# Three narrow token chunks instead of five, and one d_ff tile to two attention steps in a new order

## The chip, the core and the metric

The kernel runs on one core of a Trainium2 chip. The metric is the device time of one execution in microseconds (us). The engines are PE (TensorE, the matrix engine; PEld is its weight load), DVE (VectorE), ACT (ScalarE), POOL (GpSimd) and SP (SyncE, which issues most of the DMAs).

## What is computed

Three layers follow one another, all in float32 precision. Tokens are 4 x 576 = 2304; heads are 8 of 64 columns.

```python
def phi(x):                                   # q, k times 64 ** -0.25
    h = einsum('bhsd,md->bhsm', x, omega) - sum(x * x) / 2
    return exp(h - max(h)) / sqrt(128)
kv = einsum('bhsm,bhsd->bhmd', phi(k), v);  z = sum_s phi(k)
x = einsum('bhsm,bhmd->bhsd', phi(q), kv) / (einsum('bhsm,bhm->bhs', phi(q), z) + 1e-6)
...
h = x @ w_in                                  # d_model 512, d_ff 2048
y = (max(h, 0) + alpha * min(h, 0)) @ w_out
...
out = ((y @ w_a) * (y @ w_b)) @ w_out2        # d_ff 1536
```

## The kernel before, in words

The attention is cut into 40 key tiles: units u (four heads of one batch, 8 of them) times t (five tiles of 128 tokens, the last of 64). A step s takes one key tile and, some steps later, one query tile. Its pieces are named by their PSUM or SBUF tiles:

- `pp(u, t)`: projections of a key and a query tile (`a_proj`), then the row maxima `nm` on DVE (`a_max`) and eight exponentials `ph` on ACT (`a_exp`);
- `kv`: the state product of a key tile (`a_kv`). After a unit's fifth tile ACT copies the state to `kvp`;
- `tp`: the transposes of the features of a query tile (`a_t`), copied to `phT`;
- `nd`: numerators and denominators from `phT` and `kvp` (`a_num`), which DVE divides into `xn`;
- `xp`: transposes of `xn` (`a_x`), copied to the tokens' columns `xT`.

The second layer runs beside the attention on tokens whose `xT` is there. Its weights arrive packed; a decoder (class `Decoder`, object `D_`) unpacks them piece by piece: `r` on ACT, `a` and a custom operation on DVE, `w` on ACT, the low part on POOL. `Mlp.split` makes a high and a low part (`xh`, `xl`) of a chunk. One d_ff tile f (of 16) is `h`, 12 matmuls of 128 columns of w_in, then u, gh and gl on ACT and DVE, then `y`, 12 matmuls into the output's banks, kept for the whole chunk.

The narrow object `A` has chunks of `CI` = 256 tokens, of which there are `NCI` = 5, and does the first 8 d_ff tiles of each. The wide object `X` has chunks of 512. In phase 0 it does the first 8 d_ff tiles of the tokens that `A` leaves (`REST`), in phase 1 the last 8 tiles of all tokens. A narrow h is 12 matmuls of 256 columns, a wide one 12 of 512. The third layer follows.

The order on each engine is the order in which the program calls its parts (a manual schedule); pools of buffers add waits for what was in a buffer before. PSUM has 8 banks: five in a ring for pp, tp, nd, xp and h of the narrow part (tag "ps"), one for kv, two for y. `xn` and `phT` have two buffers each.

Steps 0 to 14 are attention alone. Then `A.run(work0, ..., stop=ALONE)` puts one attention step inside each d_ff tile, for the first `ALONE` = 4 entries of the list `work0` (chunk, its d_ff tiles). After these `group(fronts, at)` takes two attention steps and two d_ff tiles: both state products, numerators and x transposes of earlier groups come first (`wait` holds them), then the two projections, then the two feature transposes with y of the group before (`back_one`) between them, then h (`whole`). When the attention is over the rest of `line` runs alone, then `over()` makes the wide object.

Of the kernel before, what the change touches and what calls it, by code (L numbers as in the profile page):

```python
# [23 lines left out]
KT = DM // P  # L24
# [8 lines left out]
WARM = 11  # L33
Q_LAG = 6
CI = 256
NCI = 5
NF0 = 8
NFH = 5
CB = 512
REST = (512, 512)  # L40
CHUNKS = (512, 512, 256, 512, 512)
NS = 25
NS1 = 17
# [15 lines left out]
PACE2 = 1  # L59
PACE3 = 1  # L60
FIRST = 32
ALONE = 4
LAND = 5.0
SIDE = 0

# [2 lines left out]
def tile_kernel(ctx: ExitStack, tc: tile.TileContext, qT, kT, v1, omT, wbits, alpha, out):  # L68
# [411 lines left out]
    class Mlp:  # L480
        def __init__(self, st, cap, ybufs, side=None):
            self.cap = cap
            self.pair = 2 * cap <= 512
            pool = lambda **kw: st.enter_context(tc.tile_pool(side=side, reuse_waits="tile" if side else "pool", **kw))

            if not self.pair:
                self.px = pool(name=f"px{cap}", bufs=6)
            self.xs, self.ys, self.gs, self.part = {}, {}, {}, {}
            self.half = {}
            self.q = []  # L490
            self.beside = None
            self.seen = set()
            self.after = []
            self.open_ = lambda: self.rest(pool, ybufs)
            if self.pair:
                self.open_()

        def rest(self, pool, ybufs):
            cap = self.cap
            self.pg = pool(name=f"pg{cap}", bufs=3)  # L500
            self.pu = pool(name=f"pu{cap}", bufs=2 if self.pair else 1)
            self.io = pool(name=f"io{cap}", bufs=1)
            if self.pair:
                self.px = pool(name=f"px{cap}", bufs=8)
            self.banks = lambda h=None: self.open(pool, ybufs, h)

# [94 lines left out]
        def a_back(self, ph, o, n, f, last_chunk):  # L601
            halves = self.pair and o < 2 * CI
            first = f in (0, NF0) or (halves and f == NFH)
            last = f in (NF0 - 1, FA - 1) or (halves and f == NFH - 1)
            if first:
                if self.pair:
                    ts = [self.psy.tile([P, 2, 256], F32, tag="y", name=f"y{ph}_{o}_{e}") for e in range(2)]
                    self.ys[o] = [ts[e // 2][:, e % 2, :n] for e in range(KT)]
                else:
                    self.ys[o] = [self.psy.tile([P, 512], F32, tag="y", name=f"y{ph}_{o}_{e}")[:, :n]  # L610
                                  for e in range(KT)]
            ys = self.ys[o]
            wh, wl = hilo(2 * f + 1)
            gh, gl = self.gs.pop((ph, o, f))
            kinds = ((wh, gh), (wl, gh), (wh, gl))
            for e, i in [(e, i) for part in ((0, 1), (2,)) for e in range(KT) for i in part] if self.pair else \
                    [(e, i) for e in range(KT) for i in (0, 2, 1)]:
                es = slice(e * P, (e + 1) * P)
                head = not self.pair or e % 2 == 0
                tail = not self.pair or e % 2 == 1  # L620
                w_, r_ = kinds[i]
                end = 2 if self.pair else 1
                tensor.matmul(ys[e], lhsT=w_[:, es], rhs=r_,
                                 start=(first and i == 0 and head), stop=(last and i == end and tail))
                if i == end and not self.pair and e < 3 and not last:
                    D_.fill()
            D_.free[2 * f + 1] = last_chunk
            if last:
                if halves and f == NFH - 1:

                    yh = xT[:, :, 3 * S + o:3 * S + o + n]
                    for e in range(KT):
                        if e % 2:
                            vector.tensor_copy(yh[:, e], ys[e])
                        else:
                            nc.scalar.activation(yh[:, e], ys[e], AF.Copy)
                    self.half[o] = yh
                elif halves:
                    yo = self.half.pop(o)
                    for e in range(KT):  # L640
                        vector.tensor_tensor(out=yo[:, e], in0=ys[e], in1=yo[:, e], op=ALU.add)
                    nc.sync.dma_start(out=ypart[:, :, o:o + n], in_=yo)
                elif ph == 0:
                    yo = self.io.tile([P, KT, self.cap], F32, tag="io", name=f"yo{o}")[:, :, :n]
                    for e in range(KT):
                        if e % 2:
                            vector.tensor_copy(yo[:, e], ys[e])
                        else:
                            nc.scalar.activation(yo[:, e], ys[e], AF.Copy)
                    nc.sync.dma_start(out=ypart[:, :, o:o + n], in_=yo)  # L650
                else:
                    yp = self.part.pop(o)
                    for e in range(KT):
                        vector.tensor_tensor(out=yp[:, e], in0=ys[e], in1=yp[:, e], op=ALU.add)
                    nc.sync.dma_start(out=ypart[:, :, o:o + n], in_=yp)
                self.ys.pop(o)

        def load_y(self, o, n):
            yp = self.io.tile([P, KT, self.cap], F32, tag="io", name=f"yp{o}")[:, :, :n]
# [181 lines left out]
    def a_t(u, t):  # L841

        ns = slots_of(t)
        ph = phiq.pop((u, t))
        pp = bank(f"tp{u}_{t}").rearrange("p (o m) -> p o m", m=P)
        for h in range(ns):
            tensor.transpose(pp[:, h, :], ph[:, h, :], ident)
        d = pq.tile([P, 4, P], F32, tag="phT", name=f"phT{u}_{t}", bufs=2)
        if pick({"act": 0.1 + 0.13 * ns}, {"dve": 0.1 + 0.15 * ns}):
            vector.tensor_copy(d[:, :ns], pp[:, :ns])  # L850
        else:
            nc.scalar.activation(d[:, :ns], pp[:, :ns], AF.Copy)
        phT[u, t] = d
# [23 lines left out]
    def a_x(u, t, into=None):  # L877
# [10 lines left out]
            tensor.transpose(xp[:, 0, :], xn[:, 0], ident)  # L888
            xp = xp[:, 0, :].rearrange("p (a n) -> p a n", a=2)
        dst = xT[:, 2 * g:2 * g + 2, b * S + t * P:b * S + t * P + n]  # L890
        if pick({"act": 0.2 + n / 600}, {"dve": 0.1 + n / 480}):
            vector.tensor_copy(dst, xp)
        else:
            nc.scalar.activation(dst, xp, AF.Copy)
# [3 lines left out]
    done = {"kv": set(), "x": set()}  # L898
    late = {1: 3, 2: 3, 3: 4, 4: 5}
    own_banks = (0, 3, *range(6, SPLIT_AT, 2))  # L900
    held = {}
    for i, ut in enumerate((u, t) for u in range(U) for t in range(TT)):
        ev["k"][i] = ut
        ev["kv"][i + 1] = ut
# [110 lines left out]
    with st_m:  # L1015
# [38 lines left out]
        def group(fronts, at):  # L1054

            s = nxt_s[0]
            nxt_s[0] += 2
            D_.step(2 * DEC1)
            full = s < last_q
            todo = {n: wait[n][:2] for n in wait}  # L1060
            for n in wait:
                wait[n] = wait[n][2:]
            kv, t = list(todo["kv"]), list(todo["t"])
            for ut in todo["x"]:
                a_x(*ut)
            if kv:
                a_kv(*kv.pop(0))
            for ut in todo["num"]:
                a_num(*ut)
                wait["x"].append(ut)  # L1070
            if kv:
                a_kv(*kv.pop(0))
            spread(fronts, KT)
            A.flush()
            for x in (s, s + 1):
                pj = attn_1(x)
                loads(x)
                if pj:
                    a_exp(*pj, a_max(*pj))
                if x in ev["k"]:  # L1080
                    wait["kv"].append(ev["k"][x])
                if x in ev["q"]:
                    wait["t"].append(ev["q"][x])
            spread(line[at:at + 5], 2)
            D_.go(5)
            for i in range(2):
                if i < len(t):
                    a_t(*t[i])
                    wait["num"].append(t[i])
                if full:  # L1090
                    A.back_one(fronts, 2 - i)
            for w in fronts:
                A.whole(*w)
                if not full:
                    A.back_one(fronts)
            D_.go(3)

        def more():
            return nxt_s[0] < last_q or any(wait.values())
# [22 lines left out]
        def beside(ph, ci, i):  # L1122
# [13 lines left out]
            "num": [ut for ut in queries if ut in phT],  # L1136
            "x": [ut for ut in queries if ut in xns]})

        line = [(ph, o, n, f, lc) for ph, o, n, fs, lc in work0 for f in fs]

        def spread(fronts, most):
# [12 lines left out]
        while i < len(line):  # L1154
# [1 line left out]
                spread(line[i:i + 5], 2)  # L1156
            pair = []
            early = 1 if more() else 0
            for w in line[i:i + 2]:
                ph, o, n, f, _ = w  # L1160
                if all((ph, o, k) in A.xs or x_there(o + n, k, True) for k in range(KT)) and D_.ready >= 2 * f + 2 - early:
                    pair.append(w)
            if len(pair) < 2 and more():
                pair = []
            if more():
                group(pair, i)
            else:
# [6 lines left out]
        A.flush()  # L1174
        while more():
            group([], i)
        over()
        while A.q:
            A.pop()
# [338 lines left out]
```

## Time and profile before

| | us |
|---|---|
| median of 3 runs | 941.15 |
| lowest, highest | 940.59, 941.6 |
| the profiled execution: its time, its span in the trace | 941.56, 939.8 |
| PE busy | 928.4 (99% of the span) |
| DVE busy | 610.8 (65%) |
| ACT busy | 509.5 (54%) |
| POOL busy | 126.0 (13%) |

Busy times are sums of one engine's instructions in the span. A program's time is more than its span because what lies before the first and after the last instruction is in the first alone. In the rows, "idle before" is how long an engine stood, and the arrow names what released it.

### The profile page before, as it was taken

The page shows a single profiled execution, that of the slowest core. Times are in us where ns is not written, and L with a number is a line of the kernel's source. Part 1 is how long each engine was busy: PE and PEld are TensorE (multiplying, and loading weights), DVE is VectorE, ACT ScalarE, POOL GpSimd, SP SyncE. Part 2 cuts the span into 40 slices and gives each one's busy share as a digit, 9 for nine tenths or more (in the row PEclk, how much of TensorE's full clock was granted, in tenths as well). Part 3 has the DMA queues.
Part 4 walks back from the last instruction along what each step waited for, and adds up shares of the span by engine and source line. Part 5 has one row for each costly group of instructions (what it writes and reads, how often), then busy time and mean ns, then how long its engine had stood idle before and what let it go on. Part 6 is the DMA issues. An engine that isn't in the chain of part 4 may idle for free.

```text
span 939.8 us, 16686 instructions
## 1 busy us (share of the span) xinstructions
PE 928.4 (99%) x6483; PEld 842.8 (90%) x6483; DVE 610.8 (65%) x1247; ACT 509.5 (54%) x1196; POOL 126.0 (13%) x107
## 2 busy tenths in 40 slices
PE   8899999999999999999999999999999999999998
PEld 7789999999888888889888999999999898989896
DVE  5988775644567677678676796866486833374633
ACT  7878865553455554455444555655456542444541
POOL 3677700000010201000000000000011111010201
PEclk9999999999999999999999999999999999999999
DMA  9354431000234242455555856269727368333323
GB/s 333 132 208 145 149 102 50 24 1 24 90 90 135 88 159 68 167 192 196 202 180 218 309 208 234 82 211 396 285 64 239 64 188 274 102 38 97 56 46 68
DMA packets 49566, 138.92 MB, mean 148 GB/s; under 512 B 4560, under 2 KB 11088, under 8 KB 49488
## 3 DMA queue, kind: packets, MB, share of 16 engines
q1 hardware_dynamic: 44592, 129.08, 38.6%
q0 software_dynamic: 4752, 8.65, 6.4%
q8 instruction: 51, 0.84, 0.3%
q14 instruction: 27, 0.22, 0.1%
q10 hardware_dynamic: 144, 0.13, 0.0%
HBM read 90.66 MB, written 47.19 MB: 147 GB/s over the span
## 4 chain that ended last, share of the span: by engine, by line
PE 95%; ACT 2%; DVE 2%; issue 0%; ACTq 0%; DVEq 0%
PE y L191 21%; PE h L191 21%; PE W L191 16%; PE o L191 16%; PE E L191 8%; PE B L191 4%; PE tp L191 2%; ACT ph L818 2%; PE kv L191 2%; PE nd L191 2%; PE xp L191 1%; DVE xl L521 0%; DVE a L191 0%; PE warm L191 0%; DVE xn L191 0%
## 5 line engine op out<-in xcount | busy, mean ns | idle before, releaser
L191 PE MATMUL h<-xh,w 128*128 128x256 f32 (+1 forms) x768 | 189.0, 338 | 0.4 <-DVE gl L191 0.4
L191 PE MATMUL y<-gh,w 128*128 128x256 f32 (+1 forms) x768 | 184.6, 339 | 0.0
L191 PEld LDWEIGHTS h<-xh,w 128*128 128x128 f32 x768 | 125.8, 190 | 16.0 <-DVE gl L191 0.6
L191 PEld LDWEIGHTS y<-gh,w 128*128 128x128 f32 x768 | 123.3, 189 | 15.1
L191 PE MATMUL o<-w,gh 128*128 128x512 f32 x432 | 133.2, 389 | 0.0
L191 PE MATMUL h<-xl,w 128*128 128x512 f32 (+1 forms) x384 | 109.9, 337 | 0.4 <-DVE xl L521 0.4
L191 PE MATMUL y<-gl,w 128*128 128x512 f32 (+1 forms) x384 | 109.5, 336 | 0.0
L191 PEld LDWEIGHTS o<-w,gh 128*128 128x128 f32 x432 | 81.0, 188 | 16.5
L191 DVE SCALAR_TENSOR_TENSOR h<-u,bend,h 128x512 f32<-128x512 f32 (+1 forms) x72 | 47.8, 663 | 56.9 <-ACT u L555 56.8
L191 PE MATMUL o<-w,gl 128*128 128x512 f32 x216 | 84.2, 390 | 0.0
L1417 POOL DMA_DIRECT2D out<-op x30 | 26.3, 877 | 421.9 <-ACT op L166 339.7
L567 ACT ACTIVATE gh<-h 128x512 fp32r<-128x512 f32 (+1 forms) x72 | 38.0, 527 | 64.7 <-DVE h L191 64.7
L191 PEld LDWEIGHTS h<-xl,w 128*128 128x128 f32 x384 | 64.3, 190 | 8.1 <-DVE xl L521 0.6
L191 PEld LDWEIGHTS y<-gl,w 128*128 128x128 f32 x384 | 64.1, 189 | 7.4
L555 ACT ACTIVATE u<-h 128x512 f32<-128x512 f32 (+1 forms) x72 | 38.1, 529 | 56.2 <-PE h L191 51.7
L521 POOL TENSOR_TENSOR xl<-xT,xh 128x512 fp32r<-128x512 f32 (+1 forms) x16 | 20.2, 1274 | 334.5 <-ACT xh L517 334.5
L166 ACT ACTIVATE u<-W 128x384 f32<-128x384 f32 x72 | 35.3, 492 | 50.6 <-PE W L191 47.3
L166 ACT ACTIVATE op<-o 128x512 f32<-128x512 f32 x51 | 30.4, 597 | 58.2 <-PE o L191 44.8
L191 DVE TENSOR_TENSOR u<-E,u 128x384 f32<-128x384 f32 x36 | 19.6, 555 | 52.5 <-PE E L191 49.7
L191 DVE TENSOR_TENSOR gl<-h,gh 128x512 fp32r<-128x512 f32 (+1 forms) x72 | 43.1, 599 | 15.4 <-ACT gh L567 14.6
L191 DVE CUSTOM_DVE_ANT_0 a<-a,r 128x1024 uint16<-128x1024 uint16 x68 | 49.1, 723 | 4.8 <-ACT r L259 0.8
L191 PEld LDWEIGHTS o<-w,gl 128*128 128x128 f32 x216 | 40.5, 188 | 8.4
(496 smaller groups left out, 1971.9 us busy)
## 6 DMA issues: line engine op xcount, KB each, us to landing
raw<-in_w SPq DMA_DIRECT2D x68, 512.0 KB, 5.1
w<-store SPq DMA_DIRECT2D x45, 512.0 KB, 6.9
store<-t_None SPq DMA_DIRECT2D x40, 512.0 KB, 3.6
st<-ypart SPq DMA_DIRECT2D x14, 768.0 KB, 7.4
out<-op POOLq DMA_DIRECT2D x30, 256.0 KB, 5.4
q<-in_qT SPq DMA_DIRECT2D x8, 576.0 KB, 3.8
v<-in_v SPq DMA_DIRECT2D x7, 650.0 KB, 6.2
yp<-ypart SPq DMA_DIRECT2D x4, 1024.0 KB, 6.3
```

Source lines behind the costliest of these rows:

```text
L166: nc.scalar.activation(out, in_, AF.Copy)
L191: return call(*a, **k)
L521: (nc.vector, nc.gpsimd)[way].tensor_tensor(out=lo, in0=src, in1=hi.bitcast(F32), op=ALU.subtract)
L555: nc.scalar.activation(u_, hp, AF.Relu, scale=-1.0)
L567: nc.scalar.activation(gh, hp, AF.Copy)
L818: nc.scalar.activation(ph[:, 2 * pr + j], pair[j][:, o + pr], AF.Exp, bias=nm[:, j, o + pr:o + pr + 1])
L1417: nc.gpsimd.dma_start(out=dst, in_=op, accum_op=ALU.add)
```

## The change

Five narrow chunks become three and the two wide chunks of phase 0 become three, so 512 tokens' first 8 d_ff tiles move from the narrow to the wide object. The part with a step inside each d_ff tile ends after two entries of `work0` instead of four. A group has one d_ff tile beside its two steps (two tiles once no step is left), and another order: state product, numerators, state product, x transposes, projections (the gh and gl of the h before come between a tile's maxima and its exponentials), feature transposes with y between the two, then h. In groups the copies of `tp` go to DVE and those of `xp` to ACT, always. What follows the last y of a chunk (`leave`) is done later in the group.

```diff
-NCI = 5
+NCI = 3
-REST = (512, 512)
+REST = (512, 512, 512)
-ALONE = 4
+ALONE = 2
...
+            if last:
+                self.outs.append(leave)
+                if not self.hold:
+                    self.leave()
...
-        if pick({"act": 0.1 + 0.13 * ns}, {"dve": 0.1 + 0.15 * ns}):
+        if grouped or pick({"act": 0.1 + 0.13 * ns}, {"dve": 0.1 + 0.15 * ns}):
             vector.tensor_copy(d[:, :ns], pp[:, :ns])
...
-        if pick({"act": 0.2 + n / 600}, {"dve": 0.1 + n / 480}):
+        if not grouped and pick({"act": 0.2 + n / 600}, {"dve": 0.1 + n / 480}):
             vector.tensor_copy(dst, xp)
...
-            D_.step(2 * DEC1)
-            full = s < last_q
+            D_.step(DEC1)
...
-            for ut in todo["x"]:
-                a_x(*ut)
+            while first and len(xs) > 1:
+                a_x(*xs.pop(0))
             if kv:
                 a_kv(*kv.pop(0))
             for ut in todo["num"]:
...
             if kv:
                 a_kv(*kv.pop(0))
-            spread(fronts, KT)
-            A.flush()
+            for ut in xs:
+                a_x(*ut)
             for x in (s, s + 1):
                 pj = attn_1(x)
                 loads(x)
+                nm = a_max(*pj) if pj else None
+                A.flush()
                 if pj:
-                    a_exp(*pj, a_max(*pj))
+                    a_exp(*pj, nm)
...
-            spread(line[at:at + 5], 2)
-            D_.go(5)
-            for i in range(2):
-                if i < len(t):
-                    a_t(*t[i])
-                    wait["num"].append(t[i])
-                if full:
-                    A.back_one(fronts, 2 - i)
+            for i, ut in enumerate(todo["t"]):
+                a_t(*ut)
+                wait["num"].append(ut)
+                if s < last_q and not i:
+                    A.back_one(fronts, 1)
+            A.leave()
+            D_.go(3)
+            spread(fronts, KT)
             for w in fronts:
                 A.whole(*w)
-                if not full:
-                    A.back_one(fronts)
-            D_.go(3)
+                A.back_one(fronts)
+            A.leave()
+            spread(line[at:at + 5], 2)
+            D_.go()
...
-            for w in line[i:i + 2]:
+            for w in line[i:i + 1] if more() else line[i:i + 2]:
...
-            if len(pair) < 2 and more():
-                pair = []
```

On PE, from the last row that both kernels have in one place (`xp_2` of attention step 24), the kernel before goes to the h of a d_ff tile:

```order
L191 MATMUL xp_2_1851<-ident,xn_2_1732 128x128 x2
L191 MATMUL h_0_5_1855<-xh_0_0_683,w_88 128x256
...
L191 MATMUL pp(5, 0)_False_1873<-xT,k_1381 128x128
...
L191 MATMUL kv_1505<-v_1070,ph_4_1792 64x65 x8
L191 MATMUL nd_4_1917<-kvp_170,phT_4_1837 64x65 x4
```

The changed kernel goes at the same place to the state product and the numerators of its first group:

```order
L191 MATMUL xp_2_1851<-ident,xn_2_1732 128x128 x2
L191 MATMUL kv_1505<-v_1070,ph_4_1792 64x65 x8
L191 MATMUL nd_4_1864<-kvp_170,phT_4_1837 64x65 x4
L191 MATMUL xp_3_1874<-ident,xn_3_1830 128x128 x2
L191 MATMUL pp(5, 0)_False_1878<-xT,k_1381 128x128
```

The h and the projections that stood between `xp_2` and `nd_4` are gone from there.

On PE, a group in the middle (the one that projects key tiles (7, 0) and (7, 1)) reads before:

```order
L191 MATMUL xp_1_2759<-ident,xn_1_2613 128x128 x2
L191 MATMUL xp_2_2763<-ident,xn_2_2627 128x128 x2
L191 MATMUL kv_2441<-v_2088,ph_3_2658 64x65 x8
L191 MATMUL nd_3_2775<-kvp_169,phT_3_2694 64x65 x8
L191 MATMUL nd_4_2789<-kvp_169,phT_4_2713 64x65 x4
L191 MATMUL kv_2441<-v_2088,ph_4_2681 64x65 x8
L191 MATMUL pp(7, 0)_False_2816<-xT,k_2376 128x128
...
L191 MATMUL tp_2_2868<-ident,ph_2_2659 128x128 x4
L191 MATMUL y_512_0_2696<-gh_512_2_2808,w_83 128x256 x4
...
L191 MATMUL tp_3_2887<-ident,ph_3_2682 128x128 x4
L191 MATMUL y_512_0_2696<-gh_512_3_2812,w_85 128x256 x4
...
L191 MATMUL h_512_4_2906<-xh_512_0_2464,w_86 128x256
```

The same two steps in the changed kernel:

```order
L191 MATMUL kv_2345<-v_2052,ph_3_2535 64x65 x8
L191 MATMUL nd_3_2616<-kvp_169,phT_3_2571 64x65 x8
L191 MATMUL nd_4_2630<-kvp_169,phT_4_2590 64x65 x4
L191 MATMUL kv_2345<-v_2052,ph_4_2558 64x65 x8
L191 MATMUL xp_1_2649<-ident,xn_1_2486 128x128 x2
L191 MATMUL xp_2_2653<-ident,xn_2_2500 128x128 x2
L191 MATMUL pp(7, 0)_False_2657<-xT,k_2231 128x128
...
L191 MATMUL tp_2_2705<-ident,ph_2_2536 128x128 x4
L191 MATMUL y_256_0_2573<-gh_256_6_2670,w_91 128x256 x4
...
L191 MATMUL tp_3_2724<-ident,ph_3_2559 128x128 x4
L191 MATMUL h_256_7_2731<-xh_256_0_1140,w_92 128x256
```

The x transposes stand behind the state products and numerators, and one y and one h are gone from the group.

On ACT, the copy of the state of the fifth unit (`kvp_170`) stands before directly behind the exponentials of (6, 0):

```order
L818 ACTIVATE ph_0_2379<-pp(6, 0)_False_2363,nm(0, 6, 0)_2373 128x128 x2
L818 ACTIVATE ph_2_2380<-pp(6, 0)_False_2363,nm(0, 6, 0)_2373 128x128 x2
L838 ACTIVATE kvp_170<-kv_2005 128x260
L894 ACTIVATE xT<-xp_0_2433 128x2x128
L894 ACTIVATE xT<-xp_1_2437 128x2x128
```

In the changed kernel the decoder's `r` and `w`, `u` and two `xh` stand between:

```order
L831 ACTIVATE ph_0_2236<-pp(6, 0)_False_2222,nm(0, 6, 0)_2233 128x128 x2
L831 ACTIVATE ph_2_2237<-pp(6, 0)_False_2222,nm(0, 6, 0)_2233 128x128 x2
L259 ACTIVATE r_2276<-raw_2120 128x512
L590 ACTIVATE u_0_7_2295<-h_0_7_2282 128x256
L520 ACTIVATE xh_512_0_2298<-xT 128x256
L520 ACTIVATE xh_512_1_2302<-xT 128x256
L308 ACTIVATE w_94<-a_2126 128x512
L851 ACTIVATE kvp_170<-kv_1994 128x260
```

Five more instructions of ACT's queue stand ahead of the copy on which the next `nd_0` depends.

## Rows read from the trace of the kernel before

**Rows 1.** The page: busy time by engine, and the chain that ended last.

```profile
PE 928.4 (99%) x6483; PEld 842.8 (90%) x6483; DVE 610.8 (65%) x1247; ACT 509.5 (54%) x1196; POOL 126.0 (13%) x107
...
PE 95%; ACT 2%; DVE 2%; issue 0%; ACTq 0%; DVEq 0%
```

**Rows 2.** Windows: from:to, length, busy PE, PEld, DVE, ACT, POOL, PE clock, DMA.

```profile
98.98:241.90 142.92, 142.65 (x1721) 137.16 (x1720) 84.44 (x237) 81.32 (x256) 14.12 (x10) 1.00 0.15 53
282.73:326.25 43.52, 43.52 (x194) 36.04 (x192) 30.24 (x49) 24.11 (x43) 5.18 (x5) 1.00 0.35 109
...
20.00:25.00 5.00, 4.25 (x50) 3.66 (x52) 4.24 (x12) 4.86 (x17) 4.98 (x4) 0.66 0.88 325
```

**Rows 3.** PE's timeline over one group: start, length, instructions.

```profile
153.11 0.60 PE L191 MATMUL xp<-ident,xn 128*128 128x128 f32 x4
153.64 0.69 PE L191 MATMUL kv<-v,ph 128*64 128x65 f32 x16
154.16 0.87 PE L191 MATMUL nd<-kvp,phT 128*64 128x65 f32 x24
154.85 0.64 PE L191 MATMUL kv<-v,ph 128*64 128x65 f32 x16
...
157.19 0.66 PE L191 MATMUL tp<-ident,ph 128*128 128x128 f32 x4
157.60 1.20 PE L191 MATMUL y<-gh,w 128*128 128x256 f32 x8
...
159.11 0.60 PE L191 MATMUL tp<-ident,ph 128*128 128x128 f32 x4
...
160.97 0.40 PE L191 MATMUL h<-xh,w 128*128 128x256 f32 x2
...
163.85 0.38 PE L191 MATMUL xp<-ident,xn 128*128 128x128 f32 x2
```

**Rows 4.** PE's timeline where the two kernels' orders part.

```profile
98.85 0.38 PE L191 MATMUL xp<-ident,xn 128*128 128x128 f32 x2
98.98 0.72 PE L191 MATMUL h<-xh,w 128*128 128x256 f32 x4
...
100.59 0.60 PE L191 MATMUL pp(5, 0)_False<-xT,k 64*128 64x128 f32 x6
```

**Rows 5.** PE's timeline around two full numerators of a late group.

```profile
195.55 1.15 PE L191 MATMUL nd<-kvp,phT 128*64 128x65 f32 x32
196.63 0.72 PE L191 MATMUL pp(7, 2)_True<-xT,q 64*128 64x128 f32 x8
```

**Rows 6.** DVE's and ACT's timelines from 90 to 104 us.

```profile
90.55 1.29 DVE L191 TENSOR_REDUCE nm(0, 4, 3)_1688<-pp(4, 3)_False 128x4 f32<-128x512 f32 x2
...
92.80 1.02 DVE L191 CUSTOM_DVE_ANT_0 a<-a,r 128x1024 uint16<-128x1024 uint16 x1
...
102.84 1.14 DVE L191 SCALAR_TENSOR_TENSOR a<-z,a 128x512 uint32<-128x512 uint32 x1
...
91.28 2.18 ACT L818 ACTIVATE ph<-pp(4, 3)_False,nm(0, 4, 3)_1688 128x128 f32<-128x128 f32 x8 [0.42 <-DVE nm(0, 4, 3)_1688 L191]
...
99.87 0.37 ACT L852 ACTIVATE phT<-tp 128x256 f32<-128x256 f32 x1
```

**Rows 7.** Lines by form, 99 to 133 us: busy, mean ns, idle before.

```profile
L259 ACT ACTIVATE r<-raw 128x512 uint32<-128x512 uint32 x4 | 2.9, 715 | 0.0
...
L191 DVE CUSTOM_DVE_ANT_0 a<-a,r 128x1024 uint16<-128x1024 uint16 x4 | 2.8, 694 | 0.1
...
L308 ACT ACTIVATE w<-a 128x512 fp32r<-128x512 f32 x4 | 2.6, 654 | 0.3 <-DVE a L191 0.2
...
L191 DVE SCALAR_TENSOR_TENSOR a<-z,a 128x512 uint32<-128x512 uint32 x3 | 2.6, 867 | 0.0
...
L517 ACT ACTIVATE xh<-xT 128x256 fp32r<-128x256 f32 x3 | 1.1, 460 | 0.0
...
L838 ACT ACTIVATE kvp<-kv 128x260 f32<-128x260 f32 x2 | 0.9, 437 | 0.0
```

More of the change, by code (lines that the diff above doesn't have):

```diff
@@ L493, in __init__ @@
             self.after = []
+            self.outs, self.hold = [], False
             self.open_ = lambda: self.rest(pool, ybufs)
@@ L500, in rest @@
             self.pg = pool(name=f"pg{cap}", bufs=3)
+            if not self.pair:
+                self.io = pool(name=f"io{cap}", bufs=1)
             self.pu = pool(name=f"pu{cap}", bufs=2 if self.pair else 1)
-            self.io = pool(name=f"io{cap}", bufs=1)
             if self.pair:
+                self.io = pool(name=f"io{cap}", bufs=1)
                 self.px = pool(name=f"px{cap}", bufs=8)
@@ L627, in a_back, with leave @@
             D_.free[2 * f + 1] = last_chunk
-            if last:
+            def leave():
                 if halves and f == NFH - 1:
@@ L656, in a_back, with leave @@
                 self.ys.pop(o)
+            if last:
+                self.outs.append(leave)
+                if not self.hold:
+                    self.leave()
+        def leave(self):
+            while self.outs:
+                self.outs.pop(0)()
         def load_y(self, o, n):
@@ L900, in tile_kernel @@
     own_banks = (0, 3, *range(6, SPLIT_AT, 2))
-    held = {}
+    held, grouped = {}, []
     for i, ut in enumerate((u, t) for u in range(U) for t in range(TT)):
@@ L1062, in group @@
                 wait[n] = wait[n][2:]
-            kv, t = list(todo["kv"]), list(todo["t"])
-            for ut in todo["x"]:
-                a_x(*ut)
+            kv, xs = list(todo["kv"]), list(todo["x"])
+            first = at == sum(len(w[3]) for w in work0[:ALONE])
+            while first and len(xs) > 1:
+                a_x(*xs.pop(0))
             if kv:
@@ L1137, in tile_kernel @@
             "x": [ut for ut in queries if ut in xns]})
+        grouped.append(True)
+        A.hold = True
         line = [(ph, o, n, f, lc) for ph, o, n, fs, lc in work0 for f in fs]
@@ L1176, in tile_kernel @@
             group([], i)
+        A.hold = False
         over()
```

## The prediction, made before the changed kernel ran

> **What bounds the kernel now.** I read the page's busy times and its chain first: PE is busy 99% of the span and the chain that ended last is PE's for 95% of it [rows 1]. So the time is what PE has to do plus what it waits. Then the windows, over the stretch that the change touches. Both kernels issue the same instructions up to 98.98 us; from there to 241.90 runs attention beside the narrow chunks, 142.92 us in which PE is idle for 0.27 [rows 2]. Behind it lie the wide tiles. Eight of them, one chunk, take 43.52 us, and PE is busy for all of them [rows 2]. A 0.2% difference, 1.9 us, is about what a measurement of this kernel can tell from no change.
>
> **What is removed and added.** 16 of the 32 narrow y and 16 of the 30 narrow h of that stretch go; 14 h and 16 y stay. 8 wide tiles come: **+43.5 us**, PE-bound and with no decoding beside them, since the same 18 pieces are decoded before the wide part in both kernels. DVE's 30.24, ACT's 24.11 and POOL's 5.18 busy us in such a chunk [rows 2] are far from its length, so I price it at the row itself. The 16 narrow tiles that they replace cost 16 x (1.44 + 1.44) = 46.1: two h take 163.85 - 160.97 = 2.88, and a y some 1.5 where transposes stand around it [rows 3]. Half the matmuls with twice the columns save 2.6 us.
>
> The rest I price absolutely, as the sum of the changed stretch's PE blocks from starts in rows (from one block to the next, so that the switch is in the price):
>
> - kv: 16 blocks of 0.52 (153.64 to 154.16 [rows 3]) to 0.57: 8.7
> - nd: 336 matmuls, 24 in 0.69 [rows 3] or 32 in 1.08 [rows 5]: between 9.7 and 11.3, I take 10.6, since most stand as pairs of 32
> - xp: 44 transposes at 4 in 0.53 [rows 3]: 5.9
> - pp: 256 matmuls; kv and 28 of them take 157.19 - 154.85 = 2.34, less 0.57 leaves 1.77 for 28 [rows 3]: 16.2, with shorter ones 16.5
> - tp: 82 transposes, 4 in 0.41 or in 0.35 (157.19 to 157.60; 160.97 - 159.11 - 1.51) [rows 3]: 7.7
> - y: 16 at 1.51 (159.11 - 157.60 [rows 3], less 0.0 to 0.07 before an h): 24.0
> - h: 14 at 1.44 before a transpose or y [rows 3], 1.61 before a projection (100.59 - 98.98 [rows 4]): before kv, which the trace of before never shows, between these; I take 1.57, nearest the projection, which changes the tile shape likewise: 22.0
>
> That is 95.4. In the groups of before the x transposes follow h; now kv follows h and they stand between kv and pp, one change of tile shape more in each group. It is in the prices of h and xp: about 0.15 each, 2 us over 14 groups, by the 1.61 against 1.44. The Trainium skill has a rule for it (TensorEngine Tiling (Array Packing), Key Properties): changing the tiling mode, not only the tile, drains TensorE. The rows agree that it costs something, and by the rule alone, without the rows' 0.17, no sum can be made.
>
> Without waits the sum is 95.4 + 43.5 - 142.9 = **-4.0 us**. Of it 2.6 is the wide form; the rest is single steps 25 to 30, which become paired.
>
> **The waits that come.** A group in the middle now has PE work of about 0.52 + 0.69 + 0.57 + 0.53 + 1.77 + 0.41 + 1.51 + 0.35 + 1.57 = 7.9 us; before it was 10.7 (153.11 to 163.85 [rows 3]). ACT's work beside it falls only by one u, one gh: two times 8 exponentials at 2.18 [rows 6] are 4.4, the decoder's r and w 1.4, two x copies and u and gh 1.5 (0.37 each, as the copy of that shape [rows 6]), xh 0.46 to 0.9 and kvp 0.2 on the mean [rows 7]: 7.9 to 8.4. So in the groups with keys, queries and decoding (the second to about the seventh) ACT has no slack left, where it had 2 us before. That is the reason that I don't carry the small idle time of before over. I laid the rows' durations along the changed order, engine by engine:
>
> 1. First group: `xp_2` starts at 98.85; kv follows about 0.27 later (half of the 0.53 for four), and `nd_4` could start at 99.64. Its features are copied until 99.87 + 0.37 = 100.24 [rows 6], behind the decoder's w, whose 0.2 us wait on DVE shows [rows 7]. In before the h of [rows 4] lies between. Wait **0.6**.
> 2. Fourth group: `nd_0` waits for `kvp_170`. From the last projection of the third group PE has tp, y, tp, h, kv and one nd: 0.41 + 1.51 + 0.35 + 1.57 + 0.52 + 0.5 = 4.9. ACT has some 1.3 until the exponentials of (6, 0) begin (maxima at half of 1.29, and six exponentials of (5, 4) ahead), 2.18 for them [rows 6], then r 0.72, u 0.37, two xh 0.92, w 0.65, kvp 0.44 [rows 7]: 6.6. The difference is 1.7, less some 0.3 that PE already waited in the third group: **1.4**. Behind `nd_0` on PE stands everything else.
> 3. All other groups: the second projections wait for the copy of x (ACT) or for `xn` (DVE, behind the decoder's a 0.87 and custom operation 0.69 [rows 7]); h takes the bank whose exponentials end last. 0.1 to 0.5 a group in the twelve others, **3.3** in all.
>
> Together 5.3. The bounds: below, ACT's short instructions overlap as rows of before do and only the first two stay, 2; above, each decoding group repeats the fourth's, 8. That ACT's queue is served in order is the whole of item 2. The Trainium skill says so too (PSUM — Partial Sum Buffer, Engine vs sequencer instructions): ScalarE's, VectorE's and GpSimd's queues are strict FIFO; if an instruction could pass, item 2 would be 0.
>
> The sum is -4.0 + 5.3 = **+1.3 us**: 942.9 against the profiled execution's 941.56, which lies 0.4 above the median; against the median of 941.15 it is **942.5**. That is inside 0.2% (939.3 to 943.0).
>
> **Rivals.**
>
> A. The waits stay small: the chain of ACT is shorter than laid out, as in before, where 0.27 idle shows in 143 us [rows 2]. With waits of 0.8 to 2.0: 941.15 - 4.0 + 1.4 = 938.5. For it: DVE and ACT are busy 84 and 81 of 143 us there. Against it: the 7.9 of PE beside 7.9 to 8.4 of ACT. Chance 0.25.
>
> B. Slower, by one mechanism: the decoder's two DVE operations. They took 1.14 and 1.02 in places [rows 6] instead of 0.87 and 0.69; w, kvp and `xn` stand behind them. In the second to the fourth group that adds 0.6 each, 1.8: 944.3. It decides once the waits pass 5.9. For it: both long rows stand in groups of work as dense as the new ones. Against: the means are short. Chance 0.28.
>
> C. PE's clock. In 20 to 25 us, where PE was busy 4.25 of 5.00 us, the granted clock was 0.66 as a mean, a mix of its levels of 1.2 and 2.4 GHz [rows 2]; over the narrow stretch it was 1.00. If the gap of the fourth group makes it fall once for 5 us, that costs 5 x 0.34 = 1.7: 944.2. Chance 0.05.
>
> **How the numbers follow.** The forecast, 942.5 by waits of 3.4 to 5.9 us (940.6 to 943.0), has 0.42. Faster by over 0.2% (A): 0.25. Slower: B 0.28, C 0.05, together 0.33. Range: waits 2 to 8 give 939.2 to 945.2; the price of h, 14 x 0.13, and that of nd, 0.7, widen it to 938.3 and 946.0. The forecast's own range is 940.6 to 943.0.
>
> **What would show it.** From 98.85 to the first wide h 99 to 102 us, of which PE waits 4 to 6; then one wide chunk more at 43.5. `nd_4` waiting for phT at about 99.7; the longest single wait of PE at the `nd_0` behind `kvp_170`, with w in front of the copy on ACT. ACT busy above 85% from the second to the seventh group. A narrow stretch of 96 to 97 would mean rival A and that my chain on ACT is wrong; one above 103 rival B or, with a granted clock below 1.00, C. A wide chunk above 44 would break the first term.

## The result and the profile after

The changed kernel takes 953.56 us (median of 4 runs, 952.83 to 953.78) against 940.89 of before: a ratio of 1.0135, with a 95% interval of 1.0123 to 1.0147. It is 12.7 us slower, and its time lies outside the range of the prediction. The page of the changed kernel (busy times, busy tenths of the span in 40 slices, and the chain) shows one place that the page of before doesn't have:

```profile
PE 930.3 (98%) x6291; PEld 834.4 (88%) x6291; DVE 612.0 (64%) x1225; ACT 501.9 (53%) x1168; POOL 133.8 (14%) x113
...
PE   8899999999999999999999699999999999999998
...
PE 93%; ACT 3%; DVE 3%; DMA 1%; issue 0%; ACTq 0%; DVEq 0%
...
PE h L191 21%; PE y L191 20%; PE W L191 16%; PE o L191 15%; PE E L191 8%; PE B L191 4%; ACT ph L831 2%; PE nd L191 2%; PE kv L191 2%; PE tp L191 2%; DMA ypart<-yp 1%; PE xp L191 1%; DVE xl L524 0%; DVE yp L191 0%; PE warm L191 0%
```

The chain of [rows 1] had no DMA in it; now it has 1%, "ypart<-yp", and slice 23 of PE (523 to 547 us) is at six tenths. The chain between 515 and 545 us (start, length, what):

```profile
519.50 6.13 PE y L191 x27
525.63 0.02 issue
525.65 2.73 DVE yp L191 x4
528.38 0.03 DVE xl00S L191
528.41 10.76 DMA ypart<-yp
539.17 0.02 issue
539.19 0.04 ACTq L166
539.23 0.05 issue
539.27 0.50 ACT s L166
539.77 0.04 issue
539.82 4.19 PE W L191 x12
```

The last y of the second layer is added into `yp`, and the store of `yp` takes 10.76 us; ACT's copy `s` of the third layer's first result begins 0.1 us after the store's end, and PE's third group of matmuls waits for that copy. ACT's row:

```profile
539.27 0.87 ACT L166 ACTIVATE s<-W 128x384 f32<-128x384 f32 x2 [14.87 <-DMA ypart<-yp]
```

The windows of PE's wait and of what follows it (columns as in [rows 2]):

```profile
531.80:539.82 8.02, 0.05 (x2) 0.00 (x1) 0.00 (x0) 0.55 (x2) 0.00 (x0) 0.83 0.67 256
539.82:543.82 4.00, 4.00 (x12) 4.00 (x13) 2.61 (x5) 3.11 (x8) 0.00 (x0) 0.50 0.00 0
```

In the kernel before, the same 12 matmuls stand in this window:

```profile
530.34:532.41 2.07, 2.07 (x13) 2.07 (x13) 1.99 (x4) 1.70 (x4) 0.00 (x0) 1.00 1.02 394
```

PE stands 8.0 us. Then the same 12 matmuls that took 2.07 us before take 4.00, at a granted clock of 0.50 (1.2 GHz). `s` has nothing to do with `yp` as data. That it is a new buffer that lies where `yp` lay is what e1, e2 and e8 below test.

The stretch on which the prediction spoke has about the length that it said. The three windows are the narrow part from `xp_2` on, the added wide chunk, and the other wide tiles:

```profile
97.61:199.51 101.90, 100.42 (x1339) 93.10 (x1338) 72.22 (x197) 60.92 (x205) 14.27 (x11) 1.00 0.19 64
199.51:243.03 43.52, 43.52 (x194) 36.05 (x193) 29.68 (x49) 23.71 (x44) 5.14 (x4) 1.00 0.33 108
243.03:527.49 284.46, 284.46 (x1345) 239.36 (x1344) 187.78 (x316) 134.88 (x251) 22.83 (x18) 1.00 0.42 145
```

What lies ahead of this stretch differs by up to 1.4 us from trace to trace: the last y that both kernels have in one place starts at 97.34 in the profile of before and at 95.90 to 97.18 in the others. So I measure from that y. Up to the third layer before needs 428.81 us and the changed kernel 431.40: 2.6 more, where 1.3 was forecast. From the third layer's first matmul to the start of its last W they need 391.12 and 401.21: 10.1 more, where nothing was forecast. The sum, 12.7, is the difference of the medians.

### The profile page after: what moved, and what is told of

The parts are those of the page before. It is cut to its first block, busy times and chain, and to the rows that moved or that the text cites. A ratio compares the mean times of both kernels' runs of the same rounds, so it can differ in the third digit from the quotient of the medians.

```text
span 951.3 us, 16221 instructions
## 1 busy us (share of the span) xinstructions
PE 930.3 (98%) x6291; PEld 834.4 (88%) x6291; DVE 612.0 (64%) x1225; ACT 501.9 (53%) x1168; POOL 133.8 (14%) x113
## 4 chain that ended last, share of the span: by engine, by line
PE 93%; ACT 3%; DVE 3%; DMA 1%; issue 0%; ACTq 0%; DVEq 0%
PE h L191 21%; PE y L191 20%; PE W L191 16%; PE o L191 15%; PE E L191 8%; PE B L191 4%; ACT ph L831 2%; PE nd L191 2%; PE kv L191 2%; PE tp L191 2%; DMA ypart<-yp 1%; PE xp L191 1%; DVE xl L524 0%; DVE yp L191 0%; PE warm L191 0%
## 5 line engine op out<-in xcount | busy, mean ns | idle before, releaser
L191 PE MATMUL h<-xh,w 128*128 128x512 f32 (+1 forms) x704 | 190.9, 353 | 0.5 <-DVE gl L191 0.4
L191 PE MATMUL y<-gh,w 128*128 128x512 f32 (+1 forms) x704 | 186.7, 352 | 0.1
L191 PEld LDWEIGHTS h<-xh,w 128*128 128x128 f32 x704 | 120.7, 189 | 18.9 <-DVE gl L191 0.6
L191 PEld LDWEIGHTS y<-gh,w 128*128 128x128 f32 x704 | 119.0, 189 | 17.7 <-ACT gh L597 0.3
L191 PEld LDWEIGHTS o<-w,gh 128*128 128x128 f32 x432 | 81.0, 188 | 16.5
L191 DVE SCALAR_TENSOR_TENSOR h<-u,bend,h 128x512 f32<-128x512 f32 (+1 forms) x74 | 50.9, 688 | 68.2 <-ACT u L558 68.2
L558 ACT ACTIVATE u<-h 128x512 f32<-128x512 f32 (+1 forms) x74 | 40.4, 546 | 69.5 <-PE h L191 69.3
L524 POOL TENSOR_TENSOR xl<-xT,xh 128x512 fp32r<-128x512 f32 (+1 forms) x22 | 28.0, 1281 | 320.4 <-ACT xh L520 320.4
L191 PEld LDWEIGHTS h<-xl,w 128*128 128x128 f32 x352 | 61.5, 189 | 9.5 <-DVE xl L524 0.6
L191 PEld LDWEIGHTS y<-gl,w 128*128 128x128 f32 x352 | 61.4, 189 | 8.9 <-DVE gl L191 0.2
L191 DVE TENSOR_TENSOR gl<-h,gh 128x512 fp32r<-128x512 f32 (+1 forms) x74 | 46.1, 623 | 21.0 <-ACT gh L570 20.2
```

Source lines behind the costliest of these rows:

```text
L191: return call(*a, **k)
L524: (nc.vector, nc.gpsimd)[way].tensor_tensor(out=lo, in0=src, in1=hi.bitcast(F32), op=ALU.subtract)
L558: nc.scalar.activation(u_, hp, AF.Relu, scale=-1.0)
```

## The experiments

The first theory (M) was that the opening of the buffer `io` ahead of `pu` in the wide object, a part of the change that the diff above doesn't show, moved `io` under a buffer of the third layer. `io` takes 4 x 512 floats of a partition and `pu` 512, so the swap moves `io` by 2 KiB. The whole part is this:

```diff
             self.pg = pool(name=f"pg{cap}", bufs=3)
+            if not self.pair:
+                self.io = pool(name=f"io{cap}", bufs=1)
             self.pu = pool(name=f"pu{cap}", bufs=2 if self.pair else 1)
-            self.io = pool(name=f"io{cap}", bufs=1)
             if self.pair:
+                self.io = pool(name=f"io{cap}", bufs=1)
                 self.px = pool(name=f"px{cap}", bufs=8)
```

The rival (R) was that three wide chunks bring the last store into other transfers, wherever `io` lies.

**e1_io_behind**: the changed kernel without that part.

> The changed kernel with one part undone: the wide object opens its buffer io behind pu again, as in the kernel before. Theory M (memory): the third layer's first result s is put where io lies now, so ACT's copy waits until the last ypart store has read it; PE then stands 8.0 us and runs 4 us at a granted clock of 0.50, 2 us more. Without it 953.6 - 8.0 - 1.9 = 943.6 (942.6 to 944.6), and no wait of PE above 2 us between 520 and 560 us. Rival R: the stall belongs to the three wide chunks (the last store takes 10.8 us because other transfers now meet it), wherever io lies: 952 to 954.

Measured 945.27 us (5 runs), before 940.73 in the same session. The wait and the half clock are gone: 391.12 us in the third layer. R falls. The time is 0.7 above the range that M gave, and its trace accounts for 0.6 of it: the summary of waits from 199 to 212 us, where the wide tiles begin (engine, line, waited for; us in total, times, longest), has one that the changed kernel didn't have.

```profile
ACT u L556 <- DMA ypart<-yo: 5.1, 1, 5.1
DVE h L191 <- ACT u L556: 4.0, 1, 4.0
...
PE y L191 <- DVE gl L191: 0.2, 1, 0.2
```

With `io` behind, it is `pu` that lies where a store is still reading (`yo`, the last narrow chunk's). The wide part begins with a y of 3.35 us instead of 2.72. So the swap buys 0.6 us at the wide part's start in the changed kernel (nothing in the kernel before: 284.25 with and without it, in the table below) and costs 10.1 at its end.

**e2_io_ahead_alone**: the kernel before with the diff above and nothing else.

> The kernel before with that one part done alone: io of the wide object opened ahead of pu, five narrow chunks and the old groups. Theory M: the same stall comes, 7 to 8 us of wait and 2 us of half clock: 949 to 952. Rival R: 940 to 942, as before.

Measured 950.76 us (4 runs), 10.0 above before, inside M's range. The same row of PE and the same window stand in its trace:

```profile
537.08 0.69 PE L191 MATMUL W<-xh00S,w 128*128 128x384 f32 x1 [7.41 <-ACT s L166]
```

```profile
537.08:541.08 4.00, 4.00 (x12) 4.00 (x13) 2.62 (x5) 3.12 (x8) 0.00 (x0) 0.50 0.01 2
541.08:542.50 1.42, 1.42 (x6) 1.42 (x6) 0.00 (x0) 1.18 (x3) 0.00 (x0) 0.50 0.00 0
```

The half clock goes on for longer here: 19 matmuls start 0.32 us apart, up to 543.3 us. Neither chunks nor groups are needed for the loss.

**e8_s_elsewhere**: all of the change, and one line of the third layer moved, so that another tile lies on `io`.

```diff
+    tpa = xpool(RIGHT, name="tpa", bufs=1)
     gp = xpool(RIGHT, name="gp", bufs=1)
-    tpa = xpool(RIGHT, name="tpa", bufs=1)
     tpb = xpool(RIGHT, name="tpb", bufs=1)
```

> The changed kernel (io ahead of pu, as changed) with one line of the third layer moved: its pool of s, e and u opens ahead of that of gh and gl, so that io's place is taken by a gh that is written some 10 us later. Theory M: what costs is which tile lies on io, not when io opens: PE's 8 us wait and the 2 us at half clock go, and the first wide y doesn't wait 0.6 us as in e1_io_behind: 943.2 to 944.8. Rival: opening io early is at fault by itself (the store or its loads are issued later): 952 to 954.

Measured 943.58 us (5 runs), as M said. PE's 8 us and the half clock are gone, and so is the 0.6 at the first wide y. ACT still waits 2.5 us for the same store, now with a later u, and no matmul waits for that:

```profile
538.49 0.87 ACT L166 ACTIVATE u<-W 128x384 f32<-128x384 f32 x2 [2.45 <-DMA ypart<-yp]
```

What costs is which tile lies on a buffer that is being stored, and how soon PE needs it.

**e3_five_chunks**: e1 with the old numbers of chunks, and a call of `leave` where d_ff tiles run without steps.

```diff
-NCI = 3
+NCI = 5
-REST = (512, 512, 512)
+REST = (512, 512)
...
                     A.back_one(pair, 3)
+                    A.leave()
```

> As e1_io_behind (io behind pu), but five narrow chunks and two wide ones in phase 0, in the new groups. Theory W (the prediction's first term): 16 narrow tiles cost 46.1 us against 43.5 for 8 wide ones, so 2.6 us slower than e1_io_behind, 1.6 to 3.6. Rival: the narrow tiles fill waits or run beside nothing else, so the form is worth nothing: within 0.8 us of e1_io_behind.

Measured 946.16 us (5 runs), 0.9 above e1. That lies under theory W's range and just above the rival's. By the traces, from the common y to the third layer, it is 433.98 against 432.09, 1.9 us more. The first term (2.6) is there in part; the runs leave its size between 0.9 and 1.9.

**e6_three_chunks_old_groups**: the other half alone, the same two numbers changed in the kernel before (to 3 chunks).

> The kernel before with three narrow and three wide chunks alone, old groups, no other part of the change. Theory W (only the form counts): 2.6 us faster than before, 937.5 to 939. Rival C (cover): groups of two steps have d_ff tiles for four groups only; in the three or four groups that get none, PE has 4 to 5 us of work beside 5 to 6 us on ACT and DVE and waits 1 to 2 us in each: 941 to 946.

Measured 945.53 us (4 runs), 5.1 above before: rival C. The window in which its groups have no tile left:

```profile
175.00:202.00 27.00, 22.34 (x314) 17.52 (x309) 16.91 (x60) 15.89 (x50) 0.00 (x0) 1.00 0.01 1
```

PE stands 4.7 of 27 us. Fewer narrow tiles need one tile for each group, which is what the new groups give.

**e5_x_first**: e1 with all x transposes ahead of the state products, as before.

```diff
-            while first and len(xs) > 1:
+            while xs:
```

> As e1_io_behind, but in every group all x transposes stand ahead of the first state product, as in the kernel before. Theory S (order of the group): one change of tile shape less in a group, 0.15 us in 13 groups, and the second projections no longer wait for the copies of x just made, some 0.2 us in ten groups: 2 to 4 us faster than e1_io_behind. Rival: those waits belong to ACT's and DVE's load and come back at another place: within 0.8 us of e1_io_behind, or slower.

Measured 941.57 us (11 runs), 3.7 below e1. The narrow part is 2.6 us shorter, although `xp_3` of the first group now waits 0.9 us for `xn`. The same places of one group in PE's timelines, first in the changed kernel, then in e5:

```profile
132.03 0.64 PE L191 MATMUL h<-xh,w 128*128 128x256 f32 x4
132.59 0.69 PE L191 MATMUL kv<-v,ph 128*64 128x65 f32 x16
...
134.61 0.66 PE L191 MATMUL xp<-ident,xn 128*128 128x128 f32 x4
135.20 0.92 PE L191 MATMUL pp(6, 3)_False<-xT,k 64*128 64x128 f32 x7
...
137.28 0.66 PE L191 MATMUL tp<-ident,ph 128*128 128x128 f32 x4
```

```profile
131.75 0.64 PE L191 MATMUL h<-xh,w 128*128 128x256 f32 x4
132.23 0.60 PE L191 MATMUL xp<-ident,xn 128*128 128x128 f32 x4
...
134.77 0.71 PE L191 MATMUL pp(6, 3)_False<-xT,k 64*128 64x128 f32 x8
...
136.53 0.66 PE L191 MATMUL tp<-ident,ph 128*128 128x128 f32 x4
```

The last four matmuls of h take 0.56 ahead of kv and 0.48 ahead of xp, and the 28 of pp take 2.08 behind xp and 1.76 behind kv. The windows call PE busy 100% in both: a row reaches past the next row's start (132.03 + 0.64 against 132.59), and waits of a tenth of a us vanish in that. Starts show them.

**e4_w_behind_kvp** and **e9_w_behind_kvp_again**: item 2 of the waits, the copy of `kvp_170` behind the decoder on ACT. Both are e1 with the decoder's last call moved behind the next group's state products; e9 leaves it out in the first group and lets a tile start one piece earlier, so that r stays where it was.

```diff
             if kv:
                 a_kv(*kv.pop(0))
+            if not first:
+                D_.go()
...
             spread(line[at:at + 5], 2)
-            D_.go()
...
-            early = 1 if more() else 0
+            early = 2 if more() else 0
```

> As e1_io_behind, with the last call of the decoder in a group moved behind the next group's state products, so that one decoder instruction less of 0.7 us stands on ACT ahead of the copy of kvp_170. The prediction's item 2 (ACT's queue order makes nd_0 wait, 1.0 us in the changed kernel's trace): 0.5 to 0.9 us faster than e1_io_behind, and nd_0's wait 0.1 to 0.4. Rival: the instruction comes back at another place in the same chain: within 0.3 us.

e4 measured 945.17 us (5 runs), no gain, and `nd_0`'s wait grew to 1.43 us. My edit had slipped the whole decoder by one call: w came ahead of `kvp`, and w itself stood 1.15 us for DVE. So it took away the wrong instruction.

> As e1_io_behind, with only the decoder's w moved behind the copy of kvp_170 on ACT; r stays where it was (in e4 the whole decoder slipped by one call, so that a w that waits for DVE came ahead of kvp instead of r). Item 2 of the prediction: nd_0 waits for ACT's queue, of which w is 0.6 us; nd_0's wait falls from 0.80 to 0.1 to 0.4, the narrow stretch by 0.5 us, the time by 0.2 to 0.8. Rival: nd_0 waits just as long, since the copy of x or DVE ends last: no change.

e9 measured 943.11 us (5 runs, 943.06 to 945.04). The row of `nd_0` in the changed kernel, then in e9:

```profile
125.18 0.69 PE L191 MATMUL nd<-kvp,phT 128*64 128x65 f32 x16 [0.80 <-ACT kvp L851]
```

```profile
124.57 0.69 PE L191 MATMUL nd<-kvp,phT 128*64 128x65 f32 x16 [0.28 <-ACT kvp L849]
```

0.52 us less, and the narrow part is 0.58 shorter; the medians differ by more (2.2), but e9's own runs spread over 2.0. ACT's order at that place sets PE's time, as item 2 said.

**e7_best**, **e10_best_2** and **e11_best_3** put together what helped: e8's pools, x transposes first in all groups but the first, and in each group the second state product between the two numerators.

```diff
-            while first and len(xs) > 1:
+            while len(xs) > first:
...
             for ut in todo["num"]:
                 a_num(*ut)
                 wait["x"].append(ut)
-            if kv:
+                if kv:
+                    a_kv(*kv.pop(0))
+            while kv:
                 a_kv(*kv.pop(0))
```

> All that helped together: io ahead with s elsewhere (e8), x transposes first in every group but the first (e5), the decoder's last call behind the state products (e4), and in each group the second state product between the two numerators, which gives the copy of kvp 0.6 us more. From e5's trace: 0.6 us at the first wide y, 0.4 in the first group, 1.2 at nd_0 go away: 2.0 us faster than e5, 939.0 to 940.2 against 940.7 of before. Rival: the waits move on (the numerators wait for phT or the second xn comes too late): 940.6 to 942.

e7, with the decoder's call moved as in e4, measured 941.28 us (11 runs; before 940.42): 1.0006, 0.9997 to 1.0015. It had e4's fault, 1.68 us at `kvp`. e10 moves the call as in e9, and in the last single step puts the copy of `phT_4` ahead of the decoder:

```diff
-        if s >= SPLIT_AT:
+        if SPLIT_AT <= s < 24:
             D_.go()
         if s in ev["t"]:
             a_t(*ev["t"][s])
+        if s == 24:
+            D_.go()
```

> e7_best with w behind kvp as in e9, and in the last single step the copy of phT_4 on ACT ahead of the decoder's call. From e7's trace: 1.7 us of wait at kvp (0.88 of it w's wait for DVE, 0.5 w itself) and 0.5 at phT in the first group: 1.5 to 2.0 us less in the narrow stretch, 939.3 to 939.9. Rival: the two waits move to the next hand-over: 940.7 to 941.4, as e7.

e10 measured 939.50 us (11 runs; before 941.08): 0.9986, with an interval of 0.9977 to 0.9995. It is the one version whose gain over the kernel before, small as it is, is clear of the noise. Its windows are the narrow part from its `xp_2` on and all wide tiles:

```profile
98.69:196.63 97.94, 96.88 (x1338) 90.79 (x1337) 73.19 (x197) 60.17 (x205) 14.11 (x11) 1.00 0.20 67
196.63:524.62 327.99, 327.99 (x1539) 275.34 (x1537) 217.39 (x363) 158.77 (x294) 27.96 (x22) 1.00 0.41 141
```

e11 also moves the splits of the next chunk behind the state products (`spread(line[at:at + 4], 2)` there).

> As e10_best_2, and the splits xh of the next chunk behind the state products too, so that only r, u and two copies of x stand between the exponentials and kvp: 0.3 to 0.5 us less than e10. Rival: the splits then delay the exponentials of the same group, h waits for their bank: 0.3 us more.

e11 measured 939.91 us (11 runs): 0.9995, 0.9986 to 1.0004. The wait at `kvp` is gone, and h waits 0.17 and 0.38 us for exponentials instead, as the rival said; its narrow part is 0.1 us longer than e10's, and the 0.4 between the medians is within the spread of either.

Beside the medians, the starts in one trace of each (us; from the common y to the first wide h, from there to the third layer, and in the third layer; the sum against before's):

| kernel | narrow | wide | third layer | sum against before | medians' difference |
|---|---|---|---|---|---|
| before | 144.56 | 284.25 | 391.12 | | |
| changed | 103.41 | 327.99 | 401.21 | +12.7 | +12.7 |
| e1 | 103.46 | 328.63 | 391.12 | +3.3 | +4.5 |
| e2 | 144.56 | 284.25 | 401.64 | +10.5 | +10.0 |
| e3 | 149.17 | 284.81 | 391.12 | +5.2 | +5.4 |
| e4 | 104.02 | 328.39 | 391.76 | +4.2 | +4.8 |
| e5 | 100.83 | 329.03 | 391.12 | +1.1 | +0.8 |
| e6 | 105.58 | 327.99 | 391.12 | +4.8 | +5.1 |
| e7 | 101.20 | 327.99 | 391.12 | +0.4 | +0.9 |
| e8 | 103.39 | 327.99 | 391.12 | +2.6 | +3.2 |
| e9 | 102.88 | 328.35 | 391.12 | +2.4 | +2.0 |
| e10 | 99.45 | 327.99 | 391.12 | -1.4 | -1.6 |
| e11 | 99.57 | 327.99 | 391.12 | -1.3 | -1.2 |

The third layer of e4 is 0.64 us longer without a wait of PE in its rows; why stays open.

## Why the prediction was wrong

**The step that failed** is the sum's end: it stopped at the wide tiles and carried everything behind them over from before. I had followed PE's order, in which nothing changes there, and had read the new place of `io` as bookkeeping; it stands neither in the diff above nor in a term nor among the rivals. The runs put 10.1 of the 12.7 us there: 8.0 of wait, 1.9 of half clock, 0.2 around them. e2 shows that these lines alone are enough, and e1 and e8 that the loss goes without them or with `s` elsewhere. The order of instructions could not have shown it, since the dependency is one of addresses; the trace of before could have given a hint. There ACT waits for the very same store with a later tile, without harm:

```profile
536.93 0.87 ACT L166 ACTIVATE u<-W 128x384 f32<-128x384 f32 x2 [2.48 <-DMA ypart<-yp]
```

Moving `io` by one `pu` was enough to put it under `s`, which ACT writes some 9 us sooner and which PE waits for.

**The wide form** (2.6 us gained). The price of what is added was right: the chunk took 43.52 us to the hundredth, PE-bound. The gain was smaller: e3 measured 1.9 of the 2.6 by the traces and 0.9 by the medians.

**The narrow stretch** (99 to 102 us forecast). The length came, 101.90, but in part by luck: PE's idle column shows 1.5 us where waits of 4 to 6 were forecast. Items 1 and 2 came at their places and were smaller: `nd_4` waited for `phT` (0.43 idle, 0.6 forecast), `nd_0` for `kvp_170` with w in front of it (0.80 idle, 1.4 forecast). All else, the priced blocks with item 3, was 1.8 us longer than forecast, so that the total against before came out as 2.6 instead of 1.3 (0.2 of it in the wide tiles). Added up from start to start without the idle time, nd takes 11.9 us and pp 19.1, priced at 10.6 and 16.5. In the kernel before they already take 11.5 and 17.5, so 0.9 and 1.0 of this are prices that I had read too low, and no new wait. The rest is small hand-overs and changes of tile shape, which the runs don't part; e5 shows how much the order sets: 2.6 us go when the x transposes stand ahead of the state products. The Trainium skill's rule (TensorEngine Tiling (Array Packing), Key Properties) that changing the mode drains TensorE agrees with the 0.56 against 0.48 at the end of h.

**The range.** The two uncertain prices behind it (14 x 0.13 for h, 0.7 for nd) add up to more than the 0.9 by which they widen it: its lower end should have been 936.7. The measured time lies outside either way.

**ACT without slack** was wrong. Two windows of the groups with keys, queries and decoding in the changed kernel:

```profile
113.00:121.00 8.00, 8.00 (x119) 7.36 (x117) 6.80 (x20) 6.61 (x24) 4.18 (x3) 1.00 0.22 73
...
130.00:138.00 8.00, 8.00 (x125) 7.48 (x124) 7.00 (x20) 5.11 (x19) 0.00 (x0) 1.00 0.38 134
```

ACT is busy 83% and 64% here and less than 83% in windows of the other groups, not above 85%; DVE, at 85% and 88%, is the fuller one. The trace of before could have warned: in the group of [rows 3] ACT was busy 7.14 of 10.70 us, so it had 3.6 us of slack there and not 2:

```profile
153.10:163.80 10.70, 10.70 (x146) 10.34 (x145) 6.50 (x17) 7.14 (x24) 0.00 (x0) 1.00 0.20 59
```

I had added up isolated lengths, but rows of ACT overlap: behind eight exponentials that start at 113.15 and take 2.22 us, `r` starts at 115.14, 2.0 us later. The waits come from the order of ACT's and DVE's queues at single places, not from a full engine; that is why e9, e5 and e10 could remove them without taking work away.

**The rivals.** A's waits came (1.5 us of idle time, 0.8 to 2.0 forecast), but not its stretch of 96 to 97 us, since the blocks were longer than priced. B's price (a longer decoder on DVE) was not what happened: in the fourth group a and the custom operation were at 0.68 and 0.69. C, the clock, was right as a mechanism and wrong in its place: 1.00 all through the narrow stretch, 0.50 behind the wait that I had not seen.

## What to carry to other kernels

A pool that opens earlier or later is a change of addresses, and with it of waits between things that share no data: for every moved buffer ask what lay there last, what lies there next, and whether a store still reads it when PE wants the place. In a diff, lines that change no instruction deserve a price like the others, above all at the seam between two stages. And where PE looks 100% busy, compare the starts of blocks in two traces: losses of 0.1 to 0.3 us at each hand-over added up to 2.6 us here, while the idle column showed 1.5 in the whole stretch.

## What the runs showed of the hardware that I had not expected

After standing for 8.0 us (changed kernel) PE ran its next 12 matmuls in 4.00 us at a granted clock of 0.50 and was back at 1.00; after standing for 7.4 us (e2) it ran its next 19 so, in 6.2 us. Waits of 1.4 us (e4) and 1.7 us (e7) at `kvp` left the granted clock of the 8 us around them at 1.00. The last store of `yp` (1 MB), issued behind four weight loads of the 3.5 us ahead of it, took 10.76 us from issue to landing, and 9.78 in the kernel before; the changed kernel's other stores of `yp` of that size took 4.42 to 5.45. No run shows whether the loads are the reason.
